# Query units by halves, a new load order and a new order table in a hedgehog attention with a gated output

## The chip, the cores and the metric

The kernel runs on one core of a Trainium2 chip. The core has a matrix engine (PE, with its weight loads shown as PEld), a vector engine (DVE), an activation engine (ACT), a general engine (POOL), and SyncE (SP), which here only issues transfers. DMA engines move data on their own; SP's transfers and POOL's go through two different queues. The metric is the device time of one execution, in microseconds (us), as the median over the runs.

## The reference

```python
def phi(x):                                   # q, k: 8 x 8 x 576 x 64, w_phi: 64 x 128
    proj = einsum('bhsd,df->bhsf', x, w_phi)
    proj = proj - max(abs(proj), axis=-1)
    return concatenate([exp(proj), exp(-proj)], axis=-1)
q_p, k_p = phi(q), phi(k)
kv = einsum('bhsf,bhsd->bhfd', k_p, v)
z = sum(k_p, axis=2)
x = einsum('bhsf,bhfd->bhsd', q_p, kv) / (einsum('bhsf,bhf->bhs', q_p, z) + 1e-6)
x = x.transpose(0, 2, 1, 3).reshape(8, 576, 512)
gate = sigmoid(causal_conv5(x, conv_w))       # per channel
out = (gate * (x @ w_val)) @ w_out            # 512 x 512 each
```

Eight batches of eight heads are independent of each other; the two weights w_val and w_out are shared.

## The kernel before

All eight batches are unrolled into about 1,060 tasks. A task is one step of one engine, such as four chunks of a projection, one exponential or one transfer. The function `build` (line 163) lists the tasks with the tasks they wait for, the engines that may run them and a planner's durations. The planner itself is not part of the program: its answer is written out in three tables. `ORDER` gives the sequence in which the tasks are recorded, and so the order on every engine; each engine takes its own tasks strictly in that order. `FLEX` names the engine where a task has a choice, and `BANKS` the PSUM banks of each group. `WARM` and `ZERO` name places in the sequence where PE gets filler matmuls without a use of their own.

One batch goes through these steps. Its 36 chunks are taken as 18 pairs and split into five `UNITS`, four of 4 pairs and one of 2.

- k: projection on PE (`kp`, line 577), absolute maxima on DVE (`kmax`, 585, tile MK), two exponentials on ACT (`kexp`, 595, tile KTIL). The maxima are not subtracted from k; they are folded into v as a factor (`ek`, 604, tile EK).
- v: POOL multiplies v by that factor (`vs`, 610 and 611, tile VT), four times per batch. PE forms the states (`st`, 620), and one of two engines copies them out (`kv`, tile KV).
- q: a projection only for the maxima (`qm` and `qmax`, 577 and 585, tile MQP), a transpose and negation of them (`mqt`, `mqr`, tile MQR), and POOL spreads them along a diagonal (`rx`, line 682, tile RX). A second projection on PE (`qp`, 693 and 698) adds the spread maxima by a matmul with ones, and ACT takes the exponentials (`qexp`, 706, tile QTIL; the short last unit 709, tile QTT).
- Output: numerators (`num`, 719 and 726), division on DVE (`nrm`, 737 and 740, tile XN), transposes (`xtp`) or, in the last two batches, transposing DMAs (`xtd`, 755, tile XT), then `gate` (781), `tanh` (785), `val` (791), `gv` (797), `out` (813 and 817), its eviction (`oev`, tile OUTS) and the store (`odma`).

Batch 0 is loaded as fp32 by SP in pieces (`load32`: four of k, five of q) and transposed on PE (`tp32`, 536), with casts on ACT or DVE (`tc32`, 542 and 544). Later batches are loaded by POOL as bf16. So that these do not disturb the first loads, POOL first copies one column of a q piece (`hold`, line 509, tile HOLD): it thereby waits until that piece has landed. The piece is number `HOLDU` = 4, the short last one. SP and POOL run their instructions in order as well; a transfer whose semaphore lane is still in use makes SP wait.

Of the kernel before, what the change touches and what calls it, by code (L numbers as in the profile page):

```python
# [26 lines left out]
QPART = ((0, 1), (2, 3, 4))  # L27
XB = (6, 7)
# [6 lines left out]
WARM = (  # L35
    "60:6:1 81:1:1 87:7:2 134:7:1 141:7:1 "
)
ZERO = "35:76:7 61:80:5 75:34:1 101:105:1 118:99:1 126:215:8 144:223:1 155:192:4 158:200:1 175:315:6 189:346:1 195:241:2 197:241:2 211:327:1"
# [41 lines left out]
)  # L80
FLEX = (
    "AAAAAADAAADDPPPPDDDDAADDDDDDDDDDDDDAAADAAAADDDDAAADDDAADAAADDADAADDDDADDDDADDDDDDAADADDAAAAAA"
)
BANKS = (
    "037362307001454523232323016701676714232367230101676012354423010145454501013660564675601456745010145450101676767014501454"
# [25 lines left out]
def dve(n, ov=0.075):  # L111
    return n / 960.0 + ov
# [50 lines left out]
def build(plan, em=None):  # L163
# [11 lines left out]
    def G(*k):  # L175
        return h.get(k)
# [188 lines left out]
class Emit:  # L365
# [535 lines left out]
```

## Time and profile before

| | us |
|---|---|
| median of 3 runs | 219.54 |
| lowest and highest | 218.94, 221.03 |
| span of the profiled execution | 217.7 |

| engine | busy us of the profiled span |
|---|---|
| PE | 195.5 |
| ACT | 180.8 |
| DVE | 170.2 |
| POOL | 132.8 |

The profile is one execution; its page gives the span from the first to the last instruction, 217.7 us, and no time of its own besides. In a group row, the columns are line, engine, operation, tiles, shapes and count, then the busy time in us and the mean ns of one, then the idle time ahead of them and what ended it. Matmuls are pipelined, so PE's busy time is more than its work.

### The profile page before, as it was taken

Reading aid. Unit: us, or ns where it says so; the run is one execution under the profiler, and the core shown is the slowest. Engines: PE = TensorE matmul, PEld = TensorE weight load, DVE = VectorE, ACT = ScalarE, POOL = GpSimd, SP = SyncE. Lnnn points to the kernel's source line nnn. Section 1 sums busy time; section 2 is a strip of 40 time slices with the busy share of each in tenths; the row PEclk is TensorE's granted clock in tenths of the full one; section 3 lists DMA queues with packets and bytes.
Section 4 is the critical chain, followed back from the end, with each engine's and each line's share of the span. In section 5 each row is a group of like instructions: output and inputs, shape, how many; then the busy total and the mean of one; then the engine's idle time right before and its main releaser. Section 6 shows DMA issues by size and latency. Waiting matters only on the chain.

```text
span 217.7 us, 9029 instructions
## 1 busy us (share of the span) xinstructions
PE 195.5 (90%) x3946; PEld 138.6 (64%) x3946; DVE 170.2 (78%) x257; ACT 180.8 (83%) x267; POOL 132.8 (61%) x172
## 2 busy tenths in 40 slices
PE   2787887778999999998999999999999999899990
PEld 2555565566676676676857776567757766687740
DVE  3199979999789988997899978998699897654510
ACT  3589999999989899998999997999988988634251
POOL 3055999897793838970999089902993879210010
PEclk9999999999999999999999999999999999999997
DMA  6999998899899799989999778969953265764166
GB/s 177 364 234 215 302 188 231 149 174 199 144 152 284 139 135 213 302 154 174 233 276 168 88 165 248 190 142 203 287 183 89 63 160 128 81 168 97 48 186 202
DMA packets 49954, 39.92 MB, mean 183 GB/s; under 512 B 34165, under 2 KB 39541, under 8 KB 49914
## 3 DMA queue, kind: packets, MB, share of 16 engines
q1 hardware_dynamic: 43616, 28.65, 55.6%
q0 software_dynamic: 6032, 10.49, 26.3%
q8 instruction: 31, 0.51, 0.9%
q10 hardware_dynamic: 266, 0.21, 0.3%
q14 instruction: 9, 0.07, 0.1%
HBM read 30.48 MB, written 9.44 MB: 183 GB/s over the span
## 4 chain that ended last, share of the span: by engine, by line
PE 52%; ACT 23%; DVE 14%; DMA 5%; issue 4%; SPq 0%; DVEq 0%; ACTq 0%
PE PS L791 11%; ACT QTIL L706 9%; PE PS L781 9%; PE PS L813 9%; ACT KTIL L595 8%; DVE MQP L585 5%; PE PS L620 5%; PE PS L577 4%; PE PS L719 4%; DVE MK L585 3%; DMA KTIL<-in_k_dram 3%; PE PS L693 2%; DMA XT<-XN 2%; PE PS L817 2%; PE PS L698 2%
## 5 line engine op out<-in xcount | busy, mean ns | idle before, releaser
L595 ACT ACTIVATE KTIL<-PS 128x1024 bf16<-128x1024 f32 (+1 forms) x80 | 71.9, 960 | 4.1 <-PE PS L577 2.0
L610 POOL TENSOR_TENSOR VT<-VN,EK 128x1152 bf16<-128x1152 f32 x32 | 67.9, 2123 | 4.0 <-ACT EK L604 3.9
L706 ACT ACTIVATE QTIL<-PS 128x1024 bf16<-128x1024 f32 x64 | 62.5, 1044 | 2.4 <-PE PS L698 1.6
L682 POOL TENSOR_TENSOR RX<-MQR,ident 128x512 bf16<-128x512 bf16 (+1 forms) x39 | 36.6, 964 | 35.7 <-DVE MQR L670 26.0
L585 DVE TENSOR_REDUCE MK<-PS 128x8 f32<-128x1024 f32 (+1 forms) x40 | 44.2, 1112 | 2.9 <-PE PS L577 1.2
L585 DVE TENSOR_REDUCE MQP<-PS 128x8 bf16<-128x1024 f32 (+1 forms) x40 | 43.6, 1112 | 3.1 <-PE PS L577 2.3
L791 PE MATMUL PS<-XT,WV 128*128 128x288 bf16 x256 | 34.8, 286 | 0.3 <-DVE GV L797 0.2
L797 DVE SCALAR_TENSOR_TENSOR GV<-TH,PS 128x576 bf16<-128x576 bf16 x32 | 23.8, 752 | 10.4 <-PE PS L791 4.7
L813 PE MATMUL PS<-WOUT,GV 128*128 128x512 bf16 x128 | 31.3, 380 | 0.0
L791 PEld LDWEIGHTS <-WV 128*128 128x128 bf16 x256 | 23.8, 98 | 7.9 <-issue 1.4
L785 ACT ACTIVATE TH<-PS 128x576 bf16<-128x576 f32 x32 | 20.3, 663 | 9.5 <-PE PS L781 6.3
L620 PE MATMUL PS<-VT,KTIL 64*128 64x65 bf16 x1152 | 23.3, 191 | 1.1 <-issue 1.0
L781 PE MATMUL PS<-XT,GW 64*64 64x288 bf16 x640 | 23.1, 285 | 0.9 <-DMA XT<-XN 0.8
L740 DVE TENSOR_TENSOR XN<-PS,RCP 128x512 bf16<-128x512 f32 x32 | 22.1, 692 | 1.5 <-DMA XT<-XN 0.4
L620 PEld LDWEIGHTS <-KTIL 64*128 64x128 bf16 x1152 | 20.8, 94 | 3.8 <-issue 2.5
L719 PEld LDWEIGHTS <-QTIL 128*128 128x128 bf16 x512 | 18.3, 97 | 6.4 <-issue 4.0
L719 PE MATMUL PS<-KV,QTIL 128*128 128x65 bf16 x512 | 20.3, 194 | 0.3 <-DVE MQP L585 0.2
L781 PEld LDWEIGHTS <-GW 64*64 64x64 bf16 x640 | 17.8, 106 | 3.3 <-DVE RCP L737 0.9
L634 ACT ACTIVATE OUTS<-PS 128x512 f32<-128x512 f32 x22 | 13.5, 619 | 7.3 <-PE PS L813 6.1
L577 PE MATMUL PS<-W,qT 64*128 64x128 bf16 x288 | 15.1, 217 | 3.7 <-ACT qT L544 0.9
L813 PEld LDWEIGHTS <-GV 128*128 128x128 bf16 x128 | 11.1, 98 | 11.3 <-issue 0.6
L577 PEld LDWEIGHTS <-qT 64*128 64x128 bf16 x288 | 10.6, 94 | 10.3 <-issue 5.2
(79 smaller groups left out, 235.6 us busy)
## 6 DMA issues: line engine op xcount, KB each, us to landing
out_dram<-OUTS SPq DMA_DIRECT2D x32, 256.0 KB, 3.4
VN<-in_v_dram SPq DMA_DIRECT2D x7, 1152.0 KB, 6.3
KQN<-in_q_dram POOLq DMA_DIRECT2D x6, 576.0 KB, 8.3
KQN<-in_k_dram POOLq DMA_DIRECT2D x6, 576.0 KB, 9.8
KTIL<-in_k_dram SPq DMA_DIRECT2D x4, 288.0 KB, 4.5
VN<-in_v_dram POOLq DMA_DIRECT2D x1, 1152.0 KB, 10.6
KTIL<-in_q_dram SPq DMA_DIRECT2D x4, 256.0 KB, 5.7
out_dram<-OUTS SPq DMA_DIRECT2D x14, 64.0 KB, 2.6
```

The lines of the kernel that those rows point to most:

```text
L577: nc.tensor.matmul(self.PS[:, t.grp.banks[par], i * P:(i + 1) * P], X[rows, (c0 + i) * P:(c0 + i + 1) * P], self.W2[rows, :], start=True, ...
L585: self.nc.vector.tensor_reduce(o, self.two(t.grp, n * P).rearrange("p a (c f) -> p a c f", f=F), AX.X, ALU.max, apply_absolute_value=True)
L595: self.nc.scalar.activation(self.KTIL[b % 2][:, s, c0:c0 + n, :, :].rearrange("p c a f -> p a c f"), self.two(t.grp, n * P).rearrange("p a ...
L610: nc.gpsimd.tensor_tensor(self.VT[g][:, s, :, 0:D], self.VN[b % 2][:, NC * g:NC * g + NC, :], e.to_broadcast([P, NC, D]), ALU.mult)
L620: nc.tensor.matmul(self.PS[:, t.grp.banks[ab], (s * 2 + x) * E1:(s * 2 + x + 1) * E1], self.KTIL[b % 2][rows, s, J // 2, J % 2, :], self.V ...
L682: self.nc.gpsimd.tensor_tensor(o, *wide(self.MQR[self.mq(b, u)][:, :], self.ident2), ALU.mult)
L706: self.nc.scalar.activation(o, i, AF.Exp, scale=1.0 - 2.0 * s)
L719: nc.tensor.matmul(self.PS[:, t.grp.banks[h // 4], (h % 4) * E1:(h % 4 + 1) * E1], Q[:, s, c % 2, h, (c // 2) * P:(c // 2 + 1) * P], self. ...
L781: self.nc.tensor.matmul(self.PS[o * D:(o + 1) * D, t.grp.banks[par], 0:R], self.GW[r, jj, 4 - m, :], X[r, 4 * a + jj, :, HALO - 8 * s:HALO ...
L791: self.nc.tensor.matmul(self.PS[:, t.grp.banks[par], 0:R], self.WV[:, i, (2 * j + par) * D:(2 * j + par + 2) * D], X[:, 4 * par + i, :, HA ...
L797: nc.vector.scalar_tensor_tensor(out=self.GV[b % 3][:, j, :, :], in0=self.TH[j][:, :, :], scalar=1.0, in1=self.two(t.grp, R), op0=ALU.add, ...
L813: nc.tensor.matmul(self.PS[:, t.grp.banks[0], :], GV[:, j, c % 2, (c // 2) * XH:(c // 2) * XH + P], self.WOUT[:, j, c % 2, :], start=(j == ...
```

## The change

- The first four query units no longer take four chunk pairs each over all heads and both halves of the runs. Units 0 and 1 together cover the first half of each run, units 2 and 3 the second (`qys`, `qp`, `rx`, `qexp`). A unit now needs two of the loaded pieces (`QNEED`), and the numerators of a half wait for the two units of that half alone, not for all five.
- The feature weights come in one transfer that repeats them over both halves of the partitions, where two transfers did so before. The convolution weights' transfer moves from ACT's queue to SP's (`c_cwl`).
- The scaling of v and the spreads of the maxima may run on POOL or DVE in every batch; before, the scaling was POOL's and only batch 0's spreads had a choice.
- For batch 1, k is loaded ahead of q.
- `ORDER`, `FLEX`, `BANKS`, `WARM` and `ZERO` are new. The fillers on zeros fall from 152 matmuls to 20. In the built program, DVE gets seven spreads and one v scaling that were POOL's.

```diff
-WARM = (
-    "60:6:1 81:1:1 87:7:2 134:7:1 141:7:1 "
-)
-ZERO = "35:76:7 61:80:5 75:34:1 101:105:1 118:99:1 126:215:8 144:223:1 155:192:4 158:200:1 175:315:6 189:346:1 195:241:2 197:241:2 211:327:1"
+QOF = {(0, 1): (0, 2), (2, 3, 4): (1, 3, 4), (0, 1, 2, 3, 4): (0, 1, 2, 3, 4)}
+QNEED = ((0, 1), (2, 3), (0, 1), (2, 3), (4,))
+WARM = "72:1:3 90:2:2 143:5:3 248:6:1"
+ZERO = "129:102:2 152:198:4"
 ORDER = (
-    "1 2 9 3 4 11 5 6 10 21 22 19 20 13 12 46 25 26 7 8 23 24 14 27 28 42 29 32 30 33 44 49 76 31 15 43 45 47 16 158 159 48 "
+    "1 2 3 4 27 28 40 41 21 22 19 20 5 9 6 7 184 8 25 26 23 11 185 29 10 158 24 178 179 42 159 160 12 161 303 45 46 304 305 "
...
-            for w in "qk":
+            for w in "kq" if b == 1 else "qk":
...
-            cc = A("mqt", 0, 0, "PE", 0.5, fn("c_cw"), [G("tp", "q", 1)], g, rank=-500)
+            cl = A("lk", 0, 0, "SP", 0.5, fn("c_cwl"), [])
+            cl = A("lk", 0, 0, "DMA", 3.0, None, [cl])
+            cc = A("mqt", 0, 0, "PE", 0.5, fn("c_cw"), [G("tp", "q", 1), cl], g, rank=-500)
...
-                h["vs", b, gi, s] = A("vs", b, gi, "POOL", 2.22, fn("vs", b, gi, s),
+                h["vs", b, gi, s] = A("vs", b, gi, ("POOL", "DVE"), (2.22, 1.36), fn("vs", b, gi, s),
...
-            for u in us:
+            for u in QOF[us]:
...
-            qp = h["qp", b, u] = A("qp", b, u, "PE", 0.118 * n, fn("qp", b, u), [rx, G("xq", b, u)], g, 1)
+            qp = h["qp", b, u] = A("qp", b, u, "PE", 0.118 * n, fn("qp", b, u), [rx] + [G("xq", b, y) for y in QNEED[u]], g, 1)
...
-        allq = [G("qexp", b, u, s) for u in range(NU) for s in range(2)] + [G("kv", b, i) for i in range(2)]
+            need = [G("qexp", b, u, s) for u in ((2 * (c // 2), 2 * (c // 2) + 1) if c < 4 else (4,)) for s in range(2)]
...
-        for i in range(2):
-            nc.scalar.dma_start(self.W32[i * D:(i + 1) * D, :], self.wphi[:, :])
+        nc.scalar.dma_start(self.W32[:, :], self.wphi[:, :].unsqueeze(0).to_broadcast([2, D, F]))
         nc.vector.tensor_copy(self.W2[:, :], self.W32[:, :])
-        nc.scalar.dma_start(self.cw5[:, :], self.wts[1][:, :])
+
+    def c_cwl(self, t):
+        self.nc.sync.dma_start(self.cw5[:, :], self.wts[1][:, :])
...
+            m = X[rows, y0 * P:(y0 + ny) * P]
+            m = m.rearrange("p (y h k x) -> p h k y x", y=ny, h=H, k=2)[:, :, u // 2] if u < 4 else m.rearrange("p (y h x) -> p h y x", y=ny, h=2 * H)
...
         if u < 4:
-            o = self.QTIL[b % 2][:, s, :, :, :].rearrange("p a h (k r) -> p a (h k) r", k=2)[:, :, :, u * 32:(u + 1) * 32]
-            self.nc.scalar.activation(o, i, AF.Exp, scale=1.0 - 2.0 * s)
+            self.nc.scalar.activation(self.QTIL[b % 2][:, s, :, :, u * D:(u + 1) * D],
+                                      self.two(t.grp, n * P).rearrange("p a (h r) -> p a h r", h=H), AF.Exp, scale=1.0 - 2.0 * s)
```

What the new table moves is seen at three places. SP at the start of the program, before (KTIL here is the tile whose space the fp32 k and q of batch 0 borrow; VN0 is v of batch 0):

```order
L527 DMA KTIL1_73<-in_k_dram 128x576 x3
L525 DMA KTIL1_73<-in_q_dram 128x512 x3
L527 DMA KTIL1_73<-in_k_dram 128x576
L525 DMA KTIL1_73<-in_q_dram 128x512
L525 DMA KTIL1_73<-in_q_dram 128x256
L531 DMA VN0_66<-in_v_dram 128x4x576
```

and now, in the changed kernel's line numbers:

```order
L531 DMA KTIL1_73<-in_k_dram 128x576 x2
L529 DMA KTIL1_73<-in_q_dram 128x256
L535 DMA VN0_66<-in_v_dram 128x4x576
L529 DMA KTIL1_73<-in_q_dram 128x512 x2
L531 DMA KTIL1_73<-in_k_dram 128x576 x2
L529 DMA KTIL1_73<-in_q_dram 128x512 x2
L460 DMA cw5_141<-in_moe_conv_w_dram 5x512
```

v of batch 0 moved from behind all pieces of k and q to the fourth place, and the short q piece, on which `hold` waits, from the last place to the third.

POOL at its first transfers, before (VN1 is v of batch 1, QTIL1 the space that the bf16 q and k of batch 1 borrow, KQN those of batch 2):

```order
L509 CAST HOLD_76<-KTIL1_73 128x1
L550 DMA QTIL1_75<-in_q_dram 128x2304
L550 DMA QTIL1_75<-in_k_dram 128x4x576
L550 DMA KQN1_65<-in_q_dram 128x2304
L550 DMA KQN0_64<-in_k_dram 128x4x576
L682 TENSOR_TENSOR RX1_135<-MQR0_90,ident2_130 128x512
L682 TENSOR_TENSOR RX0_134<-MQR0_90,ident2_130 128x512
L531 DMA VN1_67<-in_v_dram 128x4x576
```

and now:

```order
L535 DMA VN1_67<-in_v_dram 128x4x576
L513 CAST HOLD_76<-KTIL1_73 128x1
L554 DMA QTIL1_75<-in_k_dram 128x4x576
L554 DMA QTIL1_75<-in_q_dram 128x2304
L554 DMA KQN1_65<-in_q_dram 128x2304
L554 DMA KQN0_64<-in_k_dram 128x4x576
L690 TENSOR_TENSOR RX0_134<-MQR0_90,ident2_130 128x512
```

v of batch 1 moved from behind two spreads to the very front, ahead of HOLD.

DVE near the end, around batch 7's spreads, before (MK1 and MQR1 belong to batch 7, XN1 to batch 6):

```order
L585 TENSOR_REDUCE MK1_85<-PS_63 128x2x4
L628 CAST KV0_93<-PS_63 128x520
L630 TENSOR_SCALAR OUTS6_117<-PS_63 128x512
L630 TENSOR_SCALAR OUTS5_116<-PS_63 128x512
L737 RECIPROCAL RCP1_96<-PS_63 128x8
L740 TENSOR_TENSOR XN1_98<-PS_63,RCP1_96 128x512
```

and now:

```order
L589 TENSOR_REDUCE MK1_85<-PS_63 128x2x4
L635 TENSOR_SCALAR OUTS0_111<-PS_63 128x512
L635 TENSOR_SCALAR OUTS6_117<-PS_63 128x512
L696 TENSOR_TENSOR RX4_138<-MQR1_91,ident2_130 128x256
L753 RECIPROCAL RCP1_96<-PS_63 128x8
L756 TENSOR_TENSOR XN1_98<-PS_63,RCP1_96 128x512
L753 RECIPROCAL RCP0_95<-PS_63 128x8
L756 TENSOR_TENSOR XN1_98<-PS_63,RCP0_95 128x512
L615 TENSOR_TENSOR VT1_83<-VN1_67,EK_86 128x18x64
L616 CAST VT1_83<-EK_86 128x18
```

A spread and one of batch 7's v scalings now stand on DVE, among the divisions of batch 6.

More of the change, by code (lines that the diff above doesn't have):

```diff
@@ L298, in build @@
             mqr = A("mqr", b, i, "DVE", dve(128), fn("mqr", b, i), [mqt] + [G("rx", b - 2, u) for u in range(NU)], gm)
-            for u in us:
+            for u in QOF[us]:
                 n = UNITS[u][1]
-                h["rx", b, u] = A("rx", b, u, ("POOL", "DVE") if b == 0 else "POOL", (0.35 * n - 0.1, dve(n * P)) if b == 0 else 0.35 * n - 0.1,
+                h["rx", b, u] = A("rx", b, u, ("POOL", "DVE"), (0.35 * n - 0.1, dve(n * P)),
                                   fn("rx", b, u, i), [mqr, G("qp", b - 1, u)], gm if b == 0 else None)
@@ L311, in build @@
                                        , g)
-        allq = [G("qexp", b, u, s) for u in range(NU) for s in range(2)] + [G("kv", b, i) for i in range(2)]
         for c in range(5):
             g = plan.group("num", 2 if c < 4 else 1)
-            num = h["num", b, c] = A("num", b, c, "PE", 0.57 if c < 4 else 0.38, fn("num", b, c), allq,
+            need = [G("qexp", b, u, s) for u in ((2 * (c // 2), 2 * (c // 2) + 1) if c < 4 else (4,)) for s in range(2)]
+            num = h["num", b, c] = A("num", b, c, "PE", 0.57 if c < 4 else 0.38, fn("num", b, c), need + [G("kv", b, i) for i in range(2)],
                                      g, 0 if c < 4 else 2)
@@ L429, in __init__ @@
         nc.vector.tensor_scalar(self.nident2[:, :], self.ID2[:, :], -1.0, None, op0=ALU.mult)
-        self.RX = TT("RX", NU, [P, 2 * H, 4, 8])
+        self.RX = TT("RX", NU, [P, 4 * P])
         self.WV = T("WV", [P, 4, DM + D])
@@ L673, in rx, with qys @@
     def rx(self, t, b, u, i):
-        c0, n = UNITS[u]
+        y0, ny = self.qys(u)
+        nh = H if u < 4 else 2 * H
         def wide(m, e):
-            return (m.rearrange("p (h x) -> p h x", h=2 * H).unsqueeze(2).to_broadcast([P, 2 * H, n, 8]),
-                    e[:, c0:c0 + n].unsqueeze(1).unsqueeze(3).to_broadcast([P, 2 * H, n, 8]))
-        o = self.RX[u][:, :, 0:n, :]
+            m = m.rearrange("p (h k x) -> p h k x", h=H, k=2)[:, :, u // 2, :] if u < 4 else m.rearrange("p (h x) -> p h x", h=2 * H)
+            return (m.unsqueeze(2).to_broadcast([P, nh, ny, 8]),
+                    e[:, y0:y0 + ny].unsqueeze(1).unsqueeze(3).to_broadcast([P, nh, ny, 8]))
+        o = self.RX[u][:, 0:nh * ny * 8].rearrange("p (h y x) -> p h y x", h=nh, y=ny)
+        mq = self.mq(b, 2 if u in (1, 3) else 0 if u < 4 else 4)
         if t.eng == "POOL":
-            self.nc.gpsimd.tensor_tensor(o, *wide(self.MQR[self.mq(b, u)][:, :], self.ident2), ALU.mult)
-        else:
-            with self.nc.allow_low_precision("bf16 maxima"):
+            self.nc.gpsimd.tensor_tensor(o, *wide(self.MQR[mq][:, :], self.ident2), ALU.mult)
+            return
+        with self.nc.allow_low_precision("bf16 maxima"):
+            if b == 0:
                 self.nc.vector.tensor_tensor(o, *wide(self.PS[:, t.grp.banks[0], :].bitcast(BF16)[:, 0:P], self.nident2), ALU.mult)
+            else:
+                self.nc.vector.tensor_tensor(o, *wide(self.MQR[mq][:, :], self.ident2), ALU.mult)
+    def qys(self, u):
+        return (8 * (u % 2), 8) if u < 4 else UNITS[4]
     def qp(self, t, b, u):
         nc = self.nc
-        c0, n = UNITS[u]
+        y0, ny = self.qys(u)
+        w = UNITS[u][1] * P
         X = self.XT_["q"][b % 2]
```

27 lines of the change are left out of this document (14 added, 13 removed), and 70 rows, old and new, of the table ORDER.

## The prediction

> **What bounds the kernel now.** I read the page first, then the span cut into stages, then the chain and the timeline of the start, and last the single rows that price the parts.
>
> ```profile
> PE 195.5 (90%) x3946; PEld 138.6 (64%) x3946; DVE 170.2 (78%) x257; ACT 180.8 (83%) x267; POOL 132.8 (61%) x172
> PE 52%; ACT 23%; DVE 14%; DMA 5%; issue 4%; SPq 0%; DVEq 0%; ACTq 0%
> ```
>
> No engine alone explains 217.7 us: PE, ACT and DVE are all near their limit, and the chain runs over all three. The stages tell them apart (columns: stretch and its length, then busy us and instructions of PE, PEld, DVE, ACT, POOL, granted clock, DMA share, GB/s).
>
> ```profile
> 0.00:22.00 22.00, 14.65 (x175) 10.34 (x175) 13.32 (x19) 14.89 (x25) 7.59 (x21) 1.00 0.95 246
> 22.00:100.00 78.00, 69.60 (x1628) 50.86 (x1632) 68.69 (x103) 75.16 (x106) 62.05 (x70) 1.00 0.97 198
> 100.00:185.00 85.00, 84.51 (x1725) 58.93 (x1714) 75.34 (x116) 77.12 (x114) 60.43 (x73) 1.00 0.78 175
> 185.00:217.70 32.70, 26.75 (x431) 18.48 (x429) 12.90 (x23) 13.59 (x25) 2.73 (x10) 0.96 0.56 130
> ```
>
> Four stages with four limits. The first 22 us wait for the loads of batch 0. From 22 to 100 ACT is the wall: 75.16 of 78 us. From 100 to 185 PE is: 84.51 of 85. The end is PE's gates, values and outputs of batches 6 and 7, behind the last exponential. Whatever is lost in the first stage is not made good later, since ACT has 2.8 us of room in the second.
>
> **The change part by part.** *The load order at the start.* The chain of waits and the timeline of before:
>
> ```profile
> 1.67 5.58 DMA KTIL<-in_k_dram
> 4.34 0.43 SPq L527 DMA_DIRECT2D KTIL<-in_k_dram  x1
> 7.29 0.90 PE L536 MATMUL PS<-ident_f,KTIL 128*128 128x128 f32 x3 [1.21 <-DMA KTIL<-in_k_dram]
> 9.21 1.94 ACT L595 ACTIVATE KTIL<-PS 128x1024 bf16<-128x1024 f32 x2 [0.39 <-PE PS L577]
> 11.39 0.66 PE L536 MATMUL PS<-ident_f,KTIL 128*128 128x128 f32 x4
> 21.69 1.93 ACT L706 ACTIVATE QTIL<-PS 128x1024 bf16<-128x1024 f32 x2
> DMA to landing us min/median/max: 3.0/4.5/5.6
> KTIL<-in_k_dram SPq DMA_DIRECT2D x4, 288.0 KB, 4.5
> KTIL<-in_q_dram SPq DMA_DIRECT2D x4, 256.0 KB, 5.7
> VN<-in_v_dram SPq DMA_DIRECT2D x7, 1152.0 KB, 6.3
> DMA packets 270, 0.62 MB, mean 412 GB/s; under 512 B 1, under 2 KB 2, under 8 KB 270
> ```
>
> (The landing row is that of line 527, the four k pieces; the last row is SP's queue alone from 10.5 to 12 us.) Before, PE's first twelve transposes hold it until the third k piece lands at 7.25, and ACT's first exponential starts at 9.21. Now eight transposes stand ahead of the first projections, so that wait leaves the head of the line and the first two exponentials can start about 3 us sooner. What is late next is q: ACT's third instruction after them is a cast of q, and everything on ACT stands behind it. And v of batch 0, 1152 KB, now stands ahead of four q pieces and the last two k pieces.
>
> The last k piece: before it was issued at 4.34 and landed at most 5.6 later, at 9.9, with 4 x 288 + 3 x 256 = 1920 KB up to its own end. Now there are 4 x 288 + 128 + 1152 + 2 x 256 = 2944 KB. The 1024 KB more take 1.05 MB / 0.412 = 2.5 us, so it lands at 12.4. The first q piece ends 192 KB behind the old 9.9, at 10.4. The work of ACT from there:
>
> ```profile
> L544 ACT CAST kT<-PS 128x512 bf16<-128x512 f32 x4 | 2.3, 584 | 3.0 <-PE PS L536 3.0
> L544 ACT CAST qT<-PS 128x256 bf16<-128x256 f32 x1 | 0.5, 453 | 0.0
> L544 ACT CAST kT<-PS 128x256 bf16<-128x256 f32 x1 | 0.4, 403 | 0.0
> L595 ACT ACTIVATE KTIL<-PS 128x1024 bf16<-128x1024 f32 x64 | 63.5, 1050 | 2.6 <-DVE MK L585 1.3 <-PE PS L577 0.6 <-DVE GV L797 0.3
> L595 ACT ACTIVATE KTIL<-PS 128x512 bf16<-128x512 f32 x16 | 8.8, 602 | 1.5 <-PE PS L577 1.3
> L604 ACT ACTIVATE EK<-MK 128x18 f32<-128x18 f32 x4 | 0.6, 208 | 0.3 <-DVE MK L585 0.3
> ```
>
> q: 10.4 + 0.66 transposes + 0.58 cast + 2 x 0.99 exponentials (63.5/64) = 13.6. Then two k casts, the two short casts, a q cast and four exponentials: 1.17 + 0.86 + 0.58 + 3.97 = 6.6, so the first exponential of q (QTIL) starts at 20.2 against 21.69. But at that point before had done two half units and four EK exponentials (2 x 0.60 + 4 x 0.21 = 2.0) that now still stand behind it. Net: +0.5 us, not a gain. The single w_phi transfer and the gate weights' load moved from ACT's queue to SP cost nothing: one issue of some 0.43 us on SP behind the loads, and W2 is needed only after a k piece has been transposed and cast; without that cover, tenths.
>
> That sum holds if nothing else uses the DMA engines. But v of batch 1 is now POOL's first transfer, with no wait, and the HOLD that released the loads of batches 1 and 2 at 11.0 waits for the q piece that now goes third. How two queues share:
>
> ```profile
> 85.20 0.61 POOL L550 DMA_DIRECT2D KQN<-in_q_dram  x1 [0.28 <-issue]
> q1 hardware_dynamic: 379, 0.84, 98.6%
> q0 software_dynamic: 105, 0.48, 79.0%
> q1 hardware_dynamic: 132, 0.25, 24.2%
> ```
>
> (The second row is the stretch 87 to 89.5, the last two are 90 to 93.) POOL's transfer issued at 85.20 moved nothing while SP's v was in flight; once that was through, the two queues alternated almost packet for packet, and SP's kept a quarter of the engines. So POOL's v of batch 1 probably waits for what SP has already queued, and can slip in ahead of the last k piece, issued later: 1.18 MB / 0.412 = 2.9 us more. Bounds: +0.5 (none ahead) and +3.4 (all of it ahead); I take +2.0, since the row shows waiting but the last piece is issued behind it.
>
> *Work moved to DVE.* The rows, and two that show what a neighbour costs:
>
> ```profile
> L418 DVE CAST ident<-ident_f 128x128 bf16<-128x128 f32 x1 | 1.0, 987 | 0.1
> L455 DVE CAST W<-W 128x128 bf16<-128x128 f32 x1 | 0.2, 229 | 2.5 <-DMA W<-in_w_phi_dram 2.5
> L425 DVE TENSOR_TENSOR ID<-ident_f 128x64 f32<-128x64 f32 x1 | 0.8, 847 | 0.0
> L610 POOL TENSOR_TENSOR VT<-VN,EK 128x1152 bf16<-128x1152 f32 x32 | 67.9, 2123 | 4.0 <-ACT EK L604 3.9
> L682 POOL TENSOR_TENSOR RX<-MQR,ident 128x512 bf16<-128x512 bf16 x32 | 32.6, 1040 | 35.7 <-DVE MQR L670 26.0 <-DVE RCP L737 6.6 <-DVE MQR L667 3.1
> L740 DVE TENSOR_TENSOR XN<-PS,RCP 128x512 bf16<-128x512 f32 x32 | 22.1, 692 | 1.5 <-DMA XT<-XN 0.4
> L585 DVE TENSOR_REDUCE MK<-PS 128x8 f32<-128x1024 f32 x32 | 38.9, 1219 | 2.3 <-PE PS L577 1.2 <-ACT KTIL L595 0.7 <-ACT KV L632 0.2
> L630 DVE TENSOR_SCALAR OUTS<-PS 128x512 f32<-128x512 f32 x14 | 9.6, 686 | 1.6 <-PE PS L813 1.2 <-issue 0.2
> ```
>
> Seven spreads (RX) and one v scaling go to DVE, beside POOL's v scalings. Neither form is in the trace on DVE. By L740 six spreads of 512 take at most 6 x 0.69, one of 256 half of that: 4.5 us. The scaling by L585 over 1152 elements is about 1.4 us, plus its small copy. Three output evictions and two casts come to DVE and two KV casts and two small copies leave it; with 0.69 for the large ones and nothing for the small, 3 x 0.69 = 2.1 us more. DVE gains about 8 us, nearly all of it between 100 and 185, where it has 85 - 75.3 = 9.7 idle; POOL loses 9. Hidden, mostly. But the same cast took 0.99 while POOL was filling tiles and 0.23 when it was not, and a sum over 64 elements took 0.85: DVE instructions do stretch beside POOL. Below nothing: a spread off POOL shortens the wait ahead of PE's maxima by up to 1.04 - 0.69. Above: eight waits of up to one POOL scaling, 2.1 us each. I take +1.0, near the low end because PE is the wall there.
>
> The Trainium skill, page "SBUF — State Buffer", section "Who interferes with whom", says that a DVE instruction with two SBUF inputs and a GpSimd one that reads SBUF exclude each other for a whole instruction. The two stretched rows fit it; by it the eight instructions are the third rival below.
>
> *The query units by halves.* Same matmuls, same exponentials: 64-element runs instead of 32 on the write side of the q exponential, and the 1.05 and 1.04 us of L595 and L706 already show no price for shorter runs.
>
> ```profile
> L706 ACT ACTIVATE QTIL<-PS 128x1024 bf16<-128x1024 f32 x64 | 62.5, 1044 | 2.4 <-PE PS L698 1.6 <-PE PS L504 0.6
> L504 PE MATMUL PS<-ONES,NIL 64*128 64x128 bf16 x140 | 5.6, 216 | 0.0
> PE PS L781 <- DMA XT<-XN: 0.8, 1, 0.8
> ACT QTT L709 <- PE PS L698: 1.3, 1, 1.3
> ```
>
> The numerators of a half no longer need all units. In the new order three more groups of matmuls stand between batch 6's last numerator and its first gate, which covers the 0.8 us that PE waits there for the transposing DMA; I take -0.5. The 132 filler matmuls that go were in holes; the granted clock of 1.00 is what they cover, and if it fell PE's early pieces would double, some tenths each.
>
> Sum on the profiled span: 217.7 + 2.0 + 1.0 - 0.5 = 220.2. The median of the runs, 219.54, lies 1.84 above this span; with that, **222.0 us**.
>
> **Rivals.** *Faster.* SP's queue drains first, so the start costs 0.5; the waits for the spread maxima (1.6 + 1.3, last fence) and the 0.8 go: 217.7 + 0.5 - 3.7 + 1.84 = 216.3. For: nothing of POOL's moved from 87 to 89.5. Against: ACT has little room to take it from 22 to 100.
>
> *Round robin at the start.* POOL's queue alternates from about 4 us on. SP has 2.5 MB left to the last k piece; at half of 0.412 that takes 12 us, at a quarter 25, against 6: +6 to +19, of which I take +6: 217.7 + 6 + 0.5 + 0.5 + 1.84 = 226.5. For: the 90 to 93 rows. Against: the 87 to 89.5 row. The Trainium skill, page "DMA: Bandwidth & Descriptors", section "Queues, rings and completion order", states such alternation between queues, a packet of descriptors at a time; by that rule this rival is the forecast. The trace agrees only after the backlog is through.
>
> *DVE as the wall.* Each of the eight waits half a POOL scaling, 1.06: 8.5 + 8 of work less 9.7 idle: +6.8 in place of +1.0, so 227.8. It decides where POOL scales v while DVE spreads, in batches 5 to 7. Against: PE's margin there is all of it.
>
> **How the numbers follow.** The forecast has 0.38, faster 0.25, round robin 0.17, DVE 0.15, anything else 0.05. One per cent, about what can be told from no change, is 217.3 to 221.7. The forecast's own range, from its bounds, is 219 to 225: 0.20 of its 0.38 lies over 221.7, the rest within; with both slow rivals that makes 0.52 slower. Of the faster rival 0.23 lies below 217.3; what is left, with the 0.05, is 0.25 for the same. Leaving out half of that rival's lower side and the far end of the two slow ones, the range is 215.8 to 228.0.
>
> **What would show it.** Right: the first exponential of k near 6 us and of q between 20 and 24, ACT idle between; spread rows on DVE between 0.4 and 0.7 us; stages 22 to 100 as long as before. Wrong: the last k piece landing before 11 us or after 17, DVE rows of 1.5 us and more, a shorter stretch from 100 to 185, or a granted clock under 1.00 before 30 us.

## The result and the profile after

| | before | after |
|---|---|---|
| median of 4 runs, us | 219.89 | 248.17 |
| lowest and highest, us | 218.94, 221.03 | 247.04, 248.84 |
| span of the profiled execution, us | 217.7 | 246.2 |

The change makes the kernel slower: the ratio of the times is 1.1326, with a 95% interval of 1.1251 to 1.1401. The forecast was 222.0 in a range that ended at 228.0. Medians in this document are over all runs of a kernel, while ratios and intervals leave out an execution that is over 1.5% above the fastest of its kernel.

First the page of after: busy time by engine, and the chain that ended last.

```profile
PE 201.5 (82%) x3798; PEld 139.6 (57%) x3817; DVE 183.9 (75%) x267; ACT 181.1 (74%) x266; POOL 127.7 (52%) x163
PE 44%; DVE 22%; DMA 12%; ACT 12%; issue 7%; SPq 0%; DVEq 0%; ACTq 0%
```

PE has 148 fewer instructions than before, most of them fillers, and yet 6 us more busy time; its granted clock, shown below, fell behind the holes. DVE gained 13.7 us where about 8 were forecast. DMA went from 5 to 12% of the chain.

The span of after in stretches (columns as before: length, busy us of PE, PEld, DVE, ACT, POOL, then the granted clock, DMA share and GB/s). The first ends where the first exponential of q starts; the last two are short pieces inside the rest.

```profile
0.00:30.60 30.60, 14.53 (x111) 9.85 (x113) 12.68 (x18) 12.24 (x16) 7.44 (x20) 1.00 0.88 234
30.60:246.20 215.60, 186.97 (x3693) 129.76 (x3705) 171.24 (x250) 168.84 (x251) 120.27 (x143) 0.96 0.72 152
86.00:96.00 10.00, 6.87 (x192) 5.05 (x186) 5.86 (x8) 5.82 (x8) 1.60 (x2) 0.83 1.10 194
150.00:165.00 15.00, 11.36 (x172) 6.21 (x173) 12.88 (x12) 9.39 (x15) 8.13 (x13) 0.77 0.52 90
```

The first stretch is 8.9 us longer than the 21.7 of before. The rest takes 215.6 against 196.0, so about 20 us are lost after the start, part of it at two places, around 90 and 155 us, where PE stops for 2.6 and 3.5 us and its clock falls. To find where, one can follow a step that every batch has once: the exponential of the maxima (EK), which closes the k side of a batch. Its start in the timeline of ACT, in us (for batch 0 the last of its rows):

| batch | 0 | 1 | 2 | 3 | 4 | 5 | 6 | 7 | span |
|---|---|---|---|---|---|---|---|---|---|
| before | 21.5 | 39.6 | 59.6 | 84.8 | 106.1 | 128.0 | 154.2 | 176.3 | 217.7 |
| after | 33.4 | 50.0 | 71.9 | 100.4 | 120.9 | 143.9 | 174.8 | 201.9 | 246.2 |
| lag | 12.0 | 10.4 | 12.3 | 15.6 | 14.8 | 16.0 | 20.5 | 25.7 | 28.5 |

The lag has steps: 12 us at the start, 3 between batches 2 and 3, 4.5 between 5 and 6, 5 between 6 and 7, 3 at the end.

**The start.** The chain of after, then the DMA queues from 4 to 7 us and from 8 to 13 us (q1 is SP's, q0 POOL's; the figures are packets, MB and the share of the engines' time), then the timeline of ACT.

```profile
6.17 15.79 DMA KTIL<-in_k_dram
22.01 0.90 PE PS L540 x3
```

```profile
q1 hardware_dynamic: 379, 0.72, 84.9%
```

```profile
q0 software_dynamic: 344, 1.15, 66.3%
q1 hardware_dynamic: 348, 0.69, 37.5%
```

```profile
7.71 1.94 ACT L599 ACTIVATE KTIL<-PS 128x1024 bf16<-128x1024 f32 x2 [0.64 <-PE PS L581]
16.07 0.59 ACT L548 CAST qT<-PS 128x512 bf16<-128x512 f32 x1 [6.42 <-PE PS L540]
22.95 0.59 ACT L548 CAST kT<-PS 128x512 bf16<-128x512 f32 x1 [4.45 <-PE PS L540]
30.64 1.05 ACT L720 ACTIVATE QTIL<-PS 128x1024 bf16<-128x1024 f32 x1
```

POOL's transfer of v of batch 1 is issued at 2.35 us and moves its first packet at 7.1. From 8 us on the two queues alternate packet for packet, 344 against 348, and as POOL's packets are the larger ones, it moves 1.15 MB while SP moves 0.69. The hold is through at 6.54 us (11.01 before), since its q piece now comes third, so the loads of batches 1 and 2 follow at once: from 13 to 22 us POOL's queue moves another 1.26 MB. The last k piece lands at 22 us, and ACT's two long waits, 6.4 and 4.5 us, are for pieces that stand behind v of batch 0 on SP's queue and beside POOL's loads.

PE was also slow in this stretch, which the granted clock does not show. The trace holds no record of the clock before 27.6 us (10.6 in the kernel before), and a stretch without a record is shown as 1.00. The same four transposes in PE's timeline, on either side of that moment:

```profile
26.33 1.06 PE L540 MATMUL PS<-ident_f,KTIL 128*128 128x128 f32 x4
28.36 0.66 PE L540 MATMUL PS<-ident_f,KTIL 128*128 128x128 f32 x4
```

PE's rows hold the chain from 22.0 to 27.4 us; at the later rate they would take some 2 us less (an estimate, 5.4 x 0.66 / 1.06 = 3.4). In the kernel before, four such transposes take 0.66 us from 11.39 us on.

**A hole without a releaser.** (A releaser is what the profile names as the end of a wait; "issue" stands where it names none.) The timeline of PE in after, and the DMA queues from 89.6 to 90.5 and, in the last row, from 90.5 to 91.5 us.

```profile
88.95 0.72 PE L625 MATMUL PS<-VT,KTIL 64*128 64x65 bf16 x34
92.27 1.11 PE L625 MATMUL PS<-VT,KTIL 64*128 64x65 bf16 x38 [2.60 <-issue]
```

```profile
q1 hardware_dynamic: 369, 0.12, 278.0%
q8 instruction: 1, 0.02, 6.5%
...
q1 hardware_dynamic: 18, 0.00, 4.5%
```

PE stops in the middle of a state, after 34 of its 72 matmuls, and waits for nothing that the profile names. At that moment a block of instructions (queue q8) is loaded beside a transposing transfer of SP's (shares above 100% mean that packets overlap in time); it lands at 91.0, and nearly nothing moves for a microsecond.

**A spread that is shut out.** The timeline of after around 155 us, all engines, cut to what matters.

```profile
152.20 2.12 POOL L615 TENSOR_TENSOR VT<-VN,EK 128x1152 bf16<-128x1152 f32 x1
...
152.85 4.71 DVE L696 TENSOR_TENSOR RX<-MQR,ident 128x512 bf16<-128x512 bf16 x1
...
154.26 0.26 POOL L616 CAST VT<-EK 128x18 bf16<-128x18 f32 x1
...
154.40 0.56 POOL L821 COPY GVT<-GV 128x128 bf16<-128x128 bf16 x2
...
154.91 2.11 POOL L615 TENSOR_TENSOR VT<-VN,EK 128x1152 bf16<-128x1152 f32 x1
...
157.49 1.21 DVE L589 TENSOR_REDUCE MQP<-PS 128x8 bf16<-128x1024 f32 x1
...
158.75 0.61 PE L581 MATMUL PS<-W,kT 64*128 64x128 bf16 x8 [3.53 <-DVE MQP L589]
```

The spread starts on DVE while POOL scales v and ends only when POOL's next scaling is through as well, 4.71 us later. The maxima behind it come late, PE idles 3.53 us, and from 150 to 165 us its clock is 0.77.

### The profile page after: what moved, and what is told of

Its sections match the earlier page's. It is cut to its first block, busy times and chain, and to the rows that moved or that the text cites. A ratio compares the mean times of both kernels' runs of the same rounds, so it can differ in the third digit from the quotient of the medians.

```text
span 246.2 us, 8732 instructions
## 1 busy us (share of the span) xinstructions
PE 201.5 (82%) x3798; PEld 139.6 (57%) x3817; DVE 183.9 (75%) x267; ACT 181.1 (74%) x266; POOL 127.7 (52%) x163
## 4 chain that ended last, share of the span: by engine, by line
PE 44%; DVE 22%; DMA 12%; ACT 12%; issue 7%; SPq 0%; DVEq 0%; ACTq 0%
PE PS L807 10%; PE PS L829 7%; DMA KTIL<-in_k_dram 6%; PE PS L797 6%; ACT KTIL L599 6%; DVE MQP L589 5%; PE PS L581 5%; PE PS L735 4%; DVE XN L756 3%; ACT QTIL L720 3%; PE PS L625 3%; DVE GV L813 3%; DVE MK L589 3%; DMA W<-in_w_phi_dram 2%; PE PS L710 2%
## 5 line engine op out<-in xcount | busy, mean ns | idle before, releaser
L615 POOL TENSOR_TENSOR VT<-VN,EK 128x1152 bf16<-128x1152 f32 x31 | 66.2, 2134 | 11.5 <-PE PS L797 6.8
L690 POOL TENSOR_TENSOR RX<-MQR,ident 128x512 bf16<-128x512 bf16 (+1 forms) x32 | 30.8, 977 | 60.2 <-DVE MQR L675 38.4
L829 PE MATMUL PS<-WOUT,GV 128*128 128x512 bf16 x111 | 32.4, 404 | 1.2 <-issue 0.4
L797 PE MATMUL PS<-XT,GW 64*64 64x288 bf16 x640 | 23.8, 285 | 1.6 <-DVE GV L813 0.7
L735 PEld LDWEIGHTS <-QTIL 128*128 128x128 bf16 x512 | 19.0, 100 | 6.0 <-issue 4.2
L540 PE MATMUL PS<-ident_f,KTIL 128*128 128x128 f32 x36 | 9.5, 416 | 14.9 <-DMA KTIL<-in_k_dram 7.7
L581 PE MATMUL PS<-W,kT 64*128 64x128 bf16 x288 | 15.4, 232 | 7.3 <-DVE MQP L589 4.3
L735 PE MATMUL PS<-KV,QTIL 128*128 128x65 bf16 x512 | 20.9, 197 | 0.5 <-DVE XN L756 0.4
L639 ACT ACTIVATE OUTS<-PS 128x512 f32<-128x512 f32 x19 | 11.5, 605 | 12.7 <-PE PS L829 7.6
## 6 DMA issues: line engine op xcount, KB each, us to landing
VN<-in_v_dram POOLq DMA_DIRECT2D x1, 1152.0 KB, 10.6
```

What stands on the lines that cost most here:

```text
L615: eng.tensor_tensor(self.VT[g][:, s, :, 0:D], self.VN[b % 2][:, NC * g:NC * g + NC, :], e.to_broadcast([P, NC, D]), ALU.mult)
L690: self.nc.gpsimd.tensor_tensor(o, *wide(self.MQR[mq][:, :], self.ident2), ALU.mult)
L735: nc.tensor.matmul(self.PS[:, t.grp.banks[h // 4], (h % 4) * E1:(h % 4 + 1) * E1], Q[:, s, c % 2, h, (c // 2) * P:(c // 2 + 1) * P], self. ...
L797: self.nc.tensor.matmul(self.PS[o * D:(o + 1) * D, t.grp.banks[par], 0:R], self.GW[r, jj, 4 - m, :], X[r, 4 * a + jj, :, HALO - 8 * s:HALO ...
L829: nc.tensor.matmul(self.PS[:, t.grp.banks[0], :], GV[:, j, c % 2, (c // 2) * XH:(c // 2) * XH + P], self.WOUT[:, j, c % 2, :], start=(j == ...
```

## The experiments

Each edit is small. Moves in the order table are written as the sequence of the transfers on a queue, since the table's numbers tell nothing; k0 to k3 and q0 to q4 are the pieces of batch 0.

### The start taken back

```diff
 SP of the changed kernel:
-k0 k1 q4 v(batch 0) q1 q0 k2 k3 q3 q2
+k0 k1 k2 q1 q0 q3 k3 q2 q4 v(batch 0)
 POOL:
-v(batch 1) hold k(batch 1) q(batch 1) q(batch 2) k(batch 2)
+hold k(batch 1) q(batch 1) q(batch 2) k(batch 2) v(batch 1)
```

> The changed kernel with the transfers of the start in the order of before: all pieces of k and q ahead of v of batch 0 on SP, v of batch 1 on POOL behind the hold and the loads of batches 1 and 2. Nothing else is moved. Theory A (the two queues share the engines from the start, and this delay is never made up): the last k piece lands near 10 us instead of 22, the first exponential of q starts at 20 to 22 instead of 30.6, and the span falls by the whole 9 us, to 235 to 239. Theory B (later stages have slack that hid part of it): the first exponential of q comes just as early, but the span falls by less than 4 us, to 242 or more.

Measured: 236.57 us, against 248.17, so 11.6 us less; the span is 234.0. The first exponential of q, in ACT's timeline of this kernel:

```profile
18.13 1.03 ACT L720 ACTIVATE QTIL<-PS 128x1024 bf16<-128x1024 f32 x1
```

Theory A holds (the span lies 1 us under its range), and the start cost more than the 9 us by which that exponential was late. The two kernels take their steps in another order here, so EK of batch 0 is the fairer mark: it starts at 20.9, against 33.4 in after and 21.5 before. Those 12.5 us reach the end almost whole: the span falls by 12.2.

### The same part of the change alone, in the kernel before

```diff
 SP of the kernel before:
-k0 k1 k2 q1 q0 q3 k3 q2 q4 v(batch 0)
+k0 k1 v(batch 0) k2 q1 q0 q3 k3 q2 q4
 POOL:
-hold ... v(batch 1)
+v(batch 1) hold ...
```

> The kernel before with one part of the change alone: v of batch 0 as SP's third transfer and v of batch 1 as POOL's first one, ahead of the hold. Theory A (the queues share from the start): the first exponential of q moves from 21.7 to 28 or later, and the time rises by 6 to 11 us, to 226 to 231. Theory B (SP's queue goes first, as forecast): the last k piece is held back by some 3 us, the time rises by 1 to 4 us.

Measured: 225.46 against 219.17, ratio 1.0283 (1.0207 to 1.0358), 6.3 us more. First exponential of q in ACT's timeline, and the queues from 4 to 13 us:

```profile
28.22 1.92 ACT L704 ACTIVATE QTIL<-PS 128x1024 bf16<-128x1024 f32 x2
```

```profile
q1 hardware_dynamic: 853, 1.81, 61.5%
q0 software_dynamic: 270, 1.18, 34.8%
```

That exponential is 6.5 us late and the time rises by 6.3, as theory A has it. A delay of the first stage is passed on whole, and the queues share in this kernel too: POOL's first packet moves at 7.0 us, and its queue takes 34.8% of the stretch all the same. One group of filler matmuls that stood next to the moved transfer moved along with it.

### The eight instructions given back to POOL

```diff
-FLEX: seven spreads (batches 3, 5, 6, 6, 7, 7, 7) and one scaling of v (batch 7): "D"
+FLEX: the same eight: "P"
```

> The changed kernel with the seven spreads and the one scaling of v that stand on DVE given back to POOL. Nothing else is moved. Theory A (a DVE instruction with two SBUF inputs is shut out while POOL works, and PE falls idle and loses its clock behind it): no spread on DVE over 1.0 us is left, the 3.5 us hole of PE at 155 and the low clock behind it go, and the span falls by 6 to 12 us, to 234 to 240. Theory B (the stretched rows lie beside other work, and what sets the time is DVE's or PE's own work): the span stays within 3 us of 246.2, or grows because POOL gets 9 us more.

Measured: 243.01 us, 5.2 less than after; span 240.2, just outside the 234 to 240 of theory A. The time between the EK exponentials of batches 5 and 6 falls from 30.8 (143.9 to 174.8) to 24.8 us (144.9 to 169.7). That one step, where the 4.71 us spread stood, is the whole 6 us of the span; the rest of the edit nets nothing. From 150 to 165 us PE is now busy:

```profile
150.00:165.00 15.00, 14.91 (x321) 9.87 (x319) 13.77 (x19) 14.38 (x22) 11.63 (x17) 1.00 0.91 141
```

### Both

The two edits above together, on the changed kernel.

> Both of the preceding edits together. If the two causes are independent, the gains add: with 9 for the start and 6 to 12 for the spreads the span is 225 to 231, still above the 217.7 of before, and what is left is named by the waits of this run. If they overlap (the holes move when the start moves), the span stays above 233.

Measured: 233.40 us, 14.8 less than after, where the two alone gave 11.6 + 5.2 = 16.8. The span of 230.9 lies at the upper end of the first case: nearly additive, and 13 us above before. Behind the first loads, the longest waits of PE in what is left were 3.6 us for q of batch 1 and the hole without a releaser, now 2.5 us. The next three kernels go at these two.

### q of batch 1 first, v of batch 4 behind the transposes

```diff
 POOL:
-k(batch 1) q(batch 1)
+q(batch 1) k(batch 1)
```

> The kernel with both edits (start and POOL) and, in addition, POOL loads q of batch 1 ahead of k of batch 1, as before; PE transposes that q first. Theory A (the wait of 3.6 us for q of batch 1 and the low clock behind it are on the path): q of batch 1 lands near 18 instead of 22 us, the wait goes below 1 us, and the span falls by 1.5 to 3.5 us from 230.9. Theory B (ACT is the wall there and has work in hand): the wait goes, but the span falls by less than 1 us.

Measured: 234.14 us, runs from 231.62 to 235.24, against 233.40, runs from 232.65 to 235.22: no gain that stands out of the runs. The profiled span fell by 1.2 us, between the two theories. q of batch 1 lands at 17.7, as expected, and its wait goes; the hole grew from 2.5 to 3.0 us and a wait of 1.9 us for a spread took its place, which is neither theory's reason.

```diff
 SP:
-v(batch 4)  transpose k(batch 4)  transpose q(batch 4)
+transpose k(batch 4)  transpose q(batch 4)  v(batch 4)
```

> The kernel with both edits and, in addition, SP issues the load of v of batch 4 behind the two transposing transfers of k and q of that batch instead of ahead of them; nothing else is moved. Theory A (PE's hole of 2.5 us at 81.6, which no wait explains, is the load of PE's next instructions, stuck behind v and the transposes in the DMA engines): the hole shrinks below 1.2 us and the span falls by 2 to 4 us from 230.9. Theory B (the hole is bound to the place in the program, not to the traffic): the hole stays at 2 to 3 us; the span falls by less than 1.5 us, or not at all.

Measured: a median of 230.15, with four runs in two pairs: 225.42 and 227.34, 232.95 and 233.33. The profile is of one of the long ones. The hole is gone in it and EK of batch 3 starts at 88.1 instead of 92.3; but between 108 and 135 us the 4 us are lost again, where an eviction on DVE waits 3.4 us for a store. Theory A holds for the hole; the time of four such runs decides nothing.

Both of these edits together:

> Both of the preceding edits on the kernel with start and spreads given back. If all four causes are independent, the gains add: 225 to 228 of span, and what is left above 217.7 lies in the order of the steps themselves, from batch 6 on. If ACT's order sets the pace, the span stays above 229.

Measured: 232.34 us, span 229.8, as in the second case, but for another reason: in its trace, too, the eviction waits for the store (3.2 us, and PE behind it 2.3 us), and PE waits 4.3 us for a spread on POOL.

### One store sooner

The store on which that eviction waits stood on SP behind the transposing transfer of k of batch 6, and that one waits until its data has been loaded. The edit is made on the kernel with v of batch 4 behind the transposes.

```diff
 SP:
-transpose k(batch 6)  store(batch 0, part 3)
+store(batch 0, part 3)  transpose k(batch 6)
```

> The kernel with start and spreads given back and v of batch 4 behind the transposes; in addition one store of batch 0's output goes out on SP ahead of the transposing transfer of k of batch 6 instead of behind it. Theory A (the runs of the preceding kernel differ because this store at times comes too late and holds an eviction on DVE): the hole of 2.5 us at 128 to 131 goes and all runs lie at 224 to 228. Theory B (the spread between its runs has another cause): runs over 231 remain.

Measured: 226.84 us, all four runs from 225.91 to 227.77. Theory A holds; four runs alone could be chance, but none of the twelve runs of two kernels built on this one, further below, is over 229.31 either. PE's state in batch 3, in this kernel's timeline:

```profile
79.25 0.72 PE L625 MATMUL PS<-VT,KTIL 64*128 64x65 bf16 x34
80.20 0.79 PE L625 MATMUL PS<-VT,KTIL 64*128 64x65 bf16 x38 [0.23 <-issue]
```

PE still stops after 34 matmuls, so the place belongs to the program; its length, 0.23 instead of 2.5 us, belongs to the traffic. Over all traces it is 1.9 to 3.0 us in the five kernels that load v of batch 4 ahead of the transposes, and at most 0.5 in those that load it behind them.

The traces also say what the place goes by and when the stop ends. The kernel before takes its steps in another order. Without its fillers (a run described below) and with them it stops in other states:

```profile
81.70 0.49 PE L618 MATMUL PS<-VT,KTIL 64*128 64x65 bf16 x19 [1.20 <-issue]
```

```profile
99.00 0.68 PE L620 MATMUL PS<-VT,KTIL 64*128 64x65 bf16 x31 [0.96 <-issue]
```

Counted in the traces, the stop stands behind 1,246 weight loads of PE in the changed kernels, behind 1,245 in the first of these two, and behind 1,757 in the second: 512 further, and as many matmuls. So the place goes by the number of instructions that PE has taken, not by the step it is at; not every such number has a stop. And in all twelve kernels that have one of these stops, of 0.23 to 3.0 us, PE goes on 1.3 to 1.6 us after a block of instructions (16 KB, on q8) has landed: in after it lands at 91.0, here at 78.7. With v of batch 4 ahead of the transposes the block comes late. That PE waits for the block fits all of these traces; no run parts it from the rest.

### The moves on SP alone, in the changed kernel

The two edits of the kernel above on SP's queue, v of batch 4 behind the transposes and one store sooner, with start and spreads left as changed.

> The changed kernel itself with the two moves on SP alone (v of batch 4 behind the transposes, one store ahead of k of batch 6); start and spreads stay as changed. Theory A (the place of v of batch 4 is a cause of its own): the hole of 2.6 us at 89.7 goes, and the span falls by 3 to 7 us from 246.2. Theory B (the hole only shows because the start is late, and the gain is lost at the spreads): less than 2 us.

Measured: 242.54 us, 5.6 less than after; EK of batch 3 starts 24.9 us behind that of batch 2 instead of 28.6. Theory A holds; of the 5.5 us of span, 3.6 come at this step, 1.2 between batches 5 and 6 and the rest at the end. Start, spreads and SP's order have thus each been taken back alone: 11.6 + 5.2 + 5.6 = 22.4, and all together gave 248.17 - 226.84 = 21.3.

### Five times the spreads on DVE

On the kernel of 226.84 us:

```diff
-FLEX: all 35 spreads of batches 1 to 7: "P"
+FLEX: all 35 spreads of batches 1 to 7: "D"
```

> The same kernel, but all 35 spreads of batches 1 to 7 on DVE instead of POOL: the suspected cost taken five times over. Theory A (a spread on DVE is shut out while POOL works, up to several us, and free only where POOL is idle): its durations fall in two groups, 0.69 us and 1 to 5 us, the latter where POOL scales v; the mean of the 28 large ones is over 1.3 us, and the time rises by over 6 us. Theory B (0.69 each, hidden beside PE): a mean of 0.69, DVE gains 22 us of work, the time rises by less than 4 us.

Measured: 251.06 us, 24.2 more than the 226.84 of the same kernel with the spreads on POOL. The groups on DVE, and one of the shut-out rows with its neighbour in the timeline:

```profile
L696 DVE TENSOR_TENSOR RX<-MQR,ident 128x512 bf16<-128x512 bf16 x28 | 25.5, 921 | 0.1
L696 DVE TENSOR_TENSOR RX<-MQR,ident 128x256 bf16<-128x256 bf16 x7 | 10.6, 1520 | 0.0
```

```profile
176.91 2.13 POOL L615 TENSOR_TENSOR VT<-VN,EK 128x1152 bf16<-128x1152 f32 x1
177.00 2.32 DVE L696 TENSOR_TENSOR RX<-MQR,ident 128x256 bf16<-128x256 bf16 x1
```

The durations fall in two groups, as theory A has it: 25 of the 35 take 0.42 to 0.73 us and nine take 1.58 to 2.32, all nine beside a scaling or the copy behind it (one takes 1.25). Three of the short ones overlap a scaling as well. But the large ones have a mean of 0.92, not 1.3 and more; the smaller spreads, which stand nearer to the scalings, have 1.52. The price is not in the shut-out alone: the spreads' 36.1 us are about 14 more than at the short durations, while DVE's busy time rose by 32 us, from 171.2 to 203.2, of which 24.2 reached the end. DVE's mean idle time, 24% of the span, hid little of it.

### Smaller parts, alone

```diff
 Kernel before:
-WARM, ZERO: 158 filler matmuls
+WARM = "", ZERO = ""
```

> The kernel before without its filler matmuls (both tables empty); they write zeros or unused banks, so nothing that is computed goes. Theory A (short idle gaps of PE lower its granted clock, and the fillers between 12 and 47 us keep it at 1.00): the granted clock falls below 0.9 in some stretch before 60 us, and the time rises by 1.5 to 5 us. Theory B (the fillers are not needed, ACT sets the pace there): the clock may fall, but the time stays within 1 us of before.

Measured: a median of 221.21 against 219.59, with a ratio of 1.005 (0.9998 to 1.0102): some 1 us, which the interval hardly tells from nothing. From 20 to 40 us:

```profile
20.00:40.00 20.00, 15.90 (x313) 11.57 (x308) 17.91 (x25) 18.66 (x29) 17.32 (x18) 0.80 0.97 227
```

The clock falls to 0.80, as theory A says, and it costs little where ACT sets the pace: between the two theories.

```diff
 Kernel before, c_w:
-        for i in range(2):
-            nc.scalar.dma_start(self.W32[i * D:(i + 1) * D, :], self.wphi[:, :])
+        nc.scalar.dma_start(self.W32[:, :], self.wphi[:, :].unsqueeze(0).to_broadcast([2, D, F]))
```

> The kernel before with one part alone: the feature weights in one transfer that repeats them. They land near 6.2 us instead of 5.2. Theory A (PE waits for the third k piece until 7.25 anyway): the time stays within 1 us. Theory B (the first projections wait for them): it rises by 1 us.

Measured: a median of 218.85 us against 219.18, with a ratio of 1.0029 (0.9988 to 1.007): theory A.

### What is left

The kernel of 226.84 us is still 7.7 above before. Two candidates were tried.

```diff
-FLEX: the one scaling of v of batch 7: "P"
+FLEX: the same one: "D"
```

> The kernel with start, spreads and the two moves on SP taken back (226.8 us), but the one scaling of v of batch 7 on DVE again, as changed. Theory A (POOL's row of four scalings sets the end, and DVE shortens it): PE's waits for VT of 2.2 us fall below 1 us and the time falls by 1 to 3 us. Theory B (the two engines shut each other out, so the row takes as long): the scaling takes over 1.7 us on DVE or stretches POOL's, and the time stays within 1 us.

Measured: 226.75 us; nothing. The timeline around the scalings:

```profile
183.98 1.52 DVE L615 TENSOR_TENSOR VT<-VN,EK 128x1152 bf16<-128x1152 f32 x1
184.25 3.24 POOL L615 TENSOR_TENSOR VT<-VN,EK 128x1152 bf16<-128x1152 f32 x1
...
185.43 2.12 DVE L616 CAST VT<-EK 128x18 bf16<-128x18 f32 x1
...
187.43 0.68 DVE L635 TENSOR_SCALAR OUTS<-PS 128x512 f32<-128x512 f32 x1
...
188.16 1.05 PE L833 MATMUL PS<-WOUT,GVT 128*64 128x512 bf16 x8 [2.12 <-DVE OUTS L635]
```

The two engines take turns here, a whole instruction at a time. DVE's scaling holds POOL's up (3.24 instead of 2.12), then POOL's holds up DVE's copy of 18 elements, which takes 2.12 instead of 0.26, and the eviction behind that copy makes PE wait 2.12 us. PE's waits for VT are gone, as theory A asks; they came back under another name, and theory B has the time.

```diff
-ZERO = "129:102:2 152:198:4"
+ZERO = "129:102:2 152:198:4 185:348:8"
```

> The same kernel of 226.8 us with 32 more filler matmuls on zeros, right ahead of PE's idle 2 us at 39 to 41 us. Theory A (the low clock behind that wait costs time): the granted clock from 40 to 48 us is 0.9 or more and the time falls by 0.7 to 2.5 us. Theory B (ACT sets the pace there): the clock rises, but the time stays within 0.7 us.

Measured: 226.59 us, as theory B has it. The stretch from 40 to 44 us, first in the kernel without the new fillers, then with them; the clock is back:

```profile
40.00:44.00 4.00, 3.04 (x38) 1.92 (x38) 2.79 (x4) 3.17 (x4) 3.99 (x5) 0.55 1.13 212
```

```profile
40.00:44.00 4.00, 2.71 (x71) 2.01 (x65) 3.73 (x5) 4.00 (x7) 4.00 (x5) 1.00 1.17 210
```

EK of batch 2 comes 0.6 us sooner, and the end does not. That the low clock costs nothing is not shown by it: in this one trace the clock is low elsewhere instead (0.59 from 20 to 24 us and 0.79 from 188 to 196, against 1.00 in both without the new fillers). So the last 7.7 us stay open (6.3 between the two profiled spans). By the EK times of the 226.84 kernel (22.3, 39.7, 62.2, 86.8, 107.2, 130.5, 155.3, 181.1, span 224.0) they lie between batches 1 and 2 (2.5 us more than before), 6 and 7 (3.8 more) and at the end (1.5 more). PE has no single long wait there; the order of its steps is what differs, and that was not tested apart from the rest. Neither were the query units by halves, which cannot be had without the new table. No version of the changed kernel beats the kernel before.

## Why the prediction was wrong

**The start, +2.0 in the sum; it measured 11.6.** This is the step that failed most. The prediction put it as "POOL's v of batch 1 probably waits for what SP has already queued". It does not: POOL's packets move from 7.1 us on, with SP's v of batch 0 in flight until some 13 us, and from 8 to 13 us they take 66.3% of the engines' time. The evidence was the transfer issued at 85.20, which moved nothing while SP's v was in flight. What that row shows may be a late start and no more: POOL's first packet came 4.5 us after the issue there (at 89.7) and 4.8 us after it in the changed kernel, where SP's queue was far from empty. (What sets that delay is open; the load issued at 11.13 in the kernel before moved its first packet at 12.6.) The row that was set against it, the two queues sharing between 90 and 93 us, was the one that carried over.

Two more terms of the start were put at nothing. The prediction names the hold that waits for the q piece that now goes third, but has no price for the loads that it lets go at 6.54 instead of 11.01 us. And it took the granted clock of 1.00 in its first stage as measured, where the trace has no record; PE's rows in after run at the slow rate until 27.6 us. How the 11.6 us divide between v, the hold and PE's rate was not tested apart; the early v alone cost 6.3 in the kernel before. The rival "round robin at the start" names the mechanism and takes the lower end of its own +6 to +19. By the rule of the Trainium skill, page "DMA: Bandwidth & Descriptors", section "Queues, rings and completion order", queues with work alternate a packet at a time; the trace agrees, with 344 packets of POOL's queue and 348 of SP's from 8 to 13 us.

**The last k piece "landing before 11 us or after 17" was to show the step wrong.** It landed at 22. The first exponential of k came at 7.71, sooner than before but not near 6: the feature weights in one transfer land at 6.16. In the kernel before, that part alone cost nothing that could be told.

**"Whatever is lost in the first stage is not made good later."** Right: 6.5 us late at the first exponential of q, 6.3 us in the time.

**The work moved to DVE, +1.0; it measured 5.2.** Rows of 1.5 us and more were to prove it wrong, and three of the seven spreads were, up to 4.71 us. The mechanism was in the third rival, "DVE as the wall", at +6.8, and so was the place, batches 5 to 7. What failed is the choice of the low end, with the work hidden in DVE's 9.7 idle us and PE as the wall. Idle time of an engine is cover only if it lies where the new instruction stands; the 4.71 us spread stood ahead of the maxima that PE then waited 3.53 us for. The Trainium skill, page "SBUF — State Buffer", section "Who interferes with whom", says that DVE and GpSimd (POOL here) share a pair of SBUF ports, that one of them shuts the other out for a whole instruction, and that whoever issues first decides. The traces agree on the whole instruction: 1.52, 3.24 and 2.12 us in turn in the last experiment but one. On the order they do not always: the spread of 152.85 had been waiting on DVE for 2 us when POOL's scaling of 154.91 went ahead of it. The prediction's two stretched rows at the start are no case of two SBUF inputs against a reader, as it says: POOL filled tiles then, the cast has one input, and the sum stood behind it in DVE's order, both ending at 2.47 us.

**SP's place for v of batch 4, not in the sum; with one store it measured 5.6.** Nothing in the prediction weighs the order of SP's transfers beyond the start, though the new table puts that load ahead of two transposes that the load must not delay. The sum moved the later stages as they were.

**The fillers, "some tenths each".** Right in kind: the clock falls after idle gaps, to 0.80 without fillers, and that is worth about 1 us, hardly told from nothing. The sign "a granted clock under 1.00 before 30 us" did come in substance, in PE's rows and not in the column of the clock. Behind the holes the clock fell too, and PE's busy time rose by 6 us although it has fewer instructions.

**The tail, -0.5.** PE's wait for the transposing transfer fell from 0.8 to 0.4 us, about the gain of the forecast; but the stretch from EK of batch 7 to the end grew from 41.4 to 44.3 us.

**How the cases were joined.** The two slow rivals were priced as alternatives, each with its own chance. Nothing tied them: both came true at once. With +6.8 in place of the +1.0 that the 226.5 of the start's rival holds, the two together give 232.3. The range ended at 228 because each was taken alone. The rest of the way to 248.17 is the start at 11.6 instead of 6, SP's order, and the 7.7 us that stay open.

## What to carry to other kernels

A load that is not needed yet, issued early on a second queue, takes its share from the loads that are; a hold that keeps it back is worth its wait. Before giving an engine more work because it has idle time, look at which instruction will stand behind it and who waits for that one, and count the shared resource as well. Rivals that do not exclude each other must be added, not only weighed.

## What the runs showed that was not expected

- A DVE instruction beside POOL's scalings of v can wait through two of them and the copies between (4.71 us for 0.68 us of work), and a copy of 18 elements can wait through one (2.12 us for 0.26).
- PE stopped at the same place of the program, after 34 of 72 matmuls, for 0.23 to 3.0 us depending on the transfers in flight. The place goes by the number of instructions: 1,245 or 1,246 weight loads in two differently ordered programs, and 512 more in a third. A block of instructions is loaded then or shortly before. PE went on 1.3 to 1.6 us after that block had landed, in all twelve kernels that stop. That it waits for the block is likely by this, and no run was made for it.
- PE's granted clock fell to 0.55 from 40 to 44 us, behind a stretch from 36 to 40 us in which PE was busy for 1.41 us; with fillers there it was busy for 2.66 and the clock stayed at 1.00. That gained nothing measurable.
- A granted clock of 1.00 at the start of a profile can mean that there is no record yet: four transposes took 1.06 us just before the first record and 0.66 us after it.
